# Two of four token groups loaded later, one more up-projection block ahead of the spectral part, and transposes dealt out singly

## The chip, the cores and the metric

The kernel runs on one core of a Trainium2 chip. The core has a matrix engine (PE in the profile; its weight loads are PEld), a vector engine (DVE), a scalar engine (ACT) and a general engine (POOL); SP does no arithmetic and issues most of the transfers. SP, POOL and ACT each have an in-order queue of instructions, and so have PE and DVE: an instruction that waits holds up all that stand behind it on the same engine. The metric is the device time of one execution in microseconds (us), as the median of several runs.

## The reference

The program computes the forward pass and all gradients of one conditioned transformer block with a spectral mixer. Sequence S = 2048, width D = 1024, hidden width F = 3584, bf16 tensors. Cut to what matters:

```
mod = (silu(c) @ w_mod)                      # six rows of D: sa, ca, ga, sb, cb, gb
h   = layernorm(x) * (1 + ca) + sa
x1  = x + ga * irfft2(rfft2(h) * (A_w_r + 1j * A_w_i))
h2  = layernorm(x1) * (1 + cb) + sb
out = x1 + gb * (gelu(layernorm(h2) @ B_w1 + B_b1) @ B_w2 + B_b2)
_out, _vjp = jax.vjp(f, A_x, A_w_r, A_w_i, B_w1, B_b1, B_w2, B_b2, c, w_mod)
return _out, *_vjp(grad_out)
```

So there are three layer norms (n1 inside h, n2 inside h2, n3 in front of the MLP), one forward and one backward two-dimensional transform, and the products of the MLP: `z = n3 @ w1`, `gelu(z) @ w2`, and backward `ph = (gb * grad_out) @ w2^T`, `gz @ w1^T`, and the two weight gradients.

## The kernel before, in words

Tokens are held in four groups of 512 (four tiles of 128 rows each). x lies in the tiles `x4s[0..3]`, grad_out in `gos[0..3]`. A group of x is loaded by `load_tok` (L142): one plain transfer of 512 KB that SP issues, and two gathers of 256 KB each that POOL issues, because half of a group's rows are taken in reversed order.

The start of the program (L356 to L372) is a list of loads on SP: x 0, the two halves of w_mod's row ca (`mod_get(1, h)`), x 1 between them, x 2, x 3, the two halves of row gb (`mod_get(5, h)`), grad_out 0, two transposed blocks of w2 (`load_w2t`), grad_out 1 to 3, two more w2 blocks. The tiles for blocks of w_mod are a ring of three, so the second half of gb waits for the first product. A modulation row half is eight matmuls of PE (`mod_block`, L273) and a copy out of PSUM.

Then come the statistics of the first layer norm: group 1 on ACT (`ln_act`), groups 0, 2 and 3 on DVE (`ln_dve`: eight bn_stats and four aggregations a group). Each ends in a Sqrt on ACT. `x_sqrt` keeps these four instructions; the Sqrt of groups 2 and 3 is tied behind the last Sin of the transform matrices (`behind(x_sqrt[k], trig_in[0])`), since Sqrt and Sin need different ACT tables. `norm_act` (L419) writes the normed rows into `fbuf`.

Next, grad_out is transposed on PE, four 128x128 pieces to a PSUM bank (`pt`, L472), and copied out scaled by gb into `gBoT`, even banks by DVE (L476), odd ones by ACT (L480). After each of the four groups come the products of the first two w2 blocks with it (`ph_part`, L450; a part is eight matmuls, a block of four parts 32 matmuls, copied out by ACT or DVE and stored to `d_ph`). There are 28 such blocks (NFC). `PH_EARLY = 7` says that blocks 0 to 7, eight in all, are placed ahead of the spectral part; the last matmul of them is `early_pe`, behind which the first spectral matmuls `pu` (L581) are tied. `gen_mats` (L540) makes the transform matrices: POOL works out indices in `gidx`, DVE masks them, ACT takes the Sin. It stands behind the products of row sa (`mod_block(0, h)`). Meanwhile DVE folds the four normed groups (L880 to L891: multiply with 1 + ca, fold the tokens, fold the columns); the spectral part needs the result of all four.

The spectral part (`spectral_core`) is a chain of products on PE and long elementwise work on DVE. The remaining ph blocks follow it in the program, and their matmuls are also set between the spectral ones. Its last step, `consume_fwd` (L901), makes from each of four groups the output of the transform, x1, the second norm and n3; DVE carries most of it. When block `N3_AT` (23) is done, group 0 of n3 is turned (L951 to L964): eight banks of four 128x128 transposes, `pn`, in the PSUM pools s and d of two banks each, copied out into `n3Ta` alternately by DVE (`dve_copy`, L848) and ACT (`s_copy`, L845). The odd copies are ordered ahead of a Sqrt (`behind(n3_sqrts[2], ...)`). Blocks 24 to 27 then run their first halves, and `z_block` begins: `pz` (L1009) takes n3Ta and w1.

The order on each engine is set in advance by a scheduler: among the instructions that it takes to be ready it issues the one earliest in the program, `tc.high_priority()` puts the copies out of PSUM first, `tc.issue_after` and `ordered()` fix an order on one engine, and `nc.any` leaves the choice between ACT and DVE to it. On the chip this order is kept whether or not it fits the real times.

Of the kernel before, what the change touches and what calls it, by code (L numbers as in the profile page):

```python
# [22 lines left out]
NDC = D // P  # L23
# [12 lines left out]
def kernel(  # L36
# [105 lines left out]
    def load_tok(t4, src, i, eng=None):  # L142
        s3 = tok_flat(src)
        ins = (eng or nc.sync).dma_start(out=tok_plain(t4, i), in_=tok_rows(s3, i, 0, D))
        for q in range(2):
            nc.gpsimd.indirect_dma_start(out=t4[:, tok_idx(i, q), :], out_offset=None, in_=s3,
                                         in_offset=bass.IndirectOffsetOnAxis(ap=xidx[:, 2 * i + q:2 * i + q + 1], axis=0))
        return ins
# [211 lines left out]
    mod_get(1, 0)  # L360
    load_tok(x4s[1], A_x, 1)
    mod_get(1, 1)
    load_tok(x4s[2], A_x, 2)
    load_tok(x4s[3], A_x, 3)
    mod_get(5, 0)
    for h in range(2):
        mod_block(1, h, wm[1, h][:])
# [10 lines left out]
    def ln_act(x4, row, i, jk):  # L378
        sv = small.tile([P, 4, 4], FP32, tag="lnsv")
        for q in range(4):  # L380
            nc.scalar.activation(out=jk[:, q, :], in_=x4[:, q, :], func=ACT.Identity, accum_out=sv[:, q, 0:1])
        nc.vector.tensor_scalar(out=sv[:, :, 1:2], in0=sv[:, :, 0:1], scalar1=-1.0 / D, scalar2=None, op0=ALU.mult)
        for q in range(4):
            nc.scalar.activation(out=jk[:, q, :], in_=x4[:, q, :], func=ACT.Square, bias=sv[:, q, 1:2], accum_out=sv[:, q, 2:3])
        ln_fin(sv[:, :, 2:3], sv[:, :, 1:2], sv[:, :, 3:4], 1.0 / D, row, i)
# [7 lines left out]
    def ln_dve(x4, row, i):  # L393
        st = small.tile([P, 4, 2, nc.vector.BN_STATS_DIM], FP32, tag="lnst", bufs=1)
        mv = small.tile([P, 4, 4], FP32, tag="lnmv")
        for q in range(4):
            for h in range(2):
                nc.vector.bn_stats(out=st[:, q, h, :], in_=x4[:, q, h * KH:(h + 1) * KH])
            nc.vector.bn_aggr(out=mv[:, q, 0:2], in_=st[:, q])
        nc.vector.tensor_scalar(out=mv[:, :, 2:3], in0=mv[:, :, 0:1], scalar1=-1.0, scalar2=None, op0=ALU.mult)  # L400
        ln_fin(mv[:, :, 1:2], mv[:, :, 2:3], mv[:, :, 3:4], 1.0, row, i)
# [23 lines left out]

    sqrt_in, norm_in = [None], [()]

    x_sqrt = []
    for i in range(4):
        if i == 1:  # L430
            ln_act(x4s[i], 0, i, fbuf[:, i])
        else:
            with tc.issue_after(u_in.ins):
                ln_dve(x4s[i], 0, i)
        x_sqrt.append(sqrt_in[0])
    for i in range(2):
        norm_act(fbuf[:, i], x4s[i], 0, i)
    pc = ps_d("pc")
# [84 lines left out]
    def trig(dst, colv, rowv, nrow, width, modn, cosine):  # L523
        idx = gidx[:, gcount[0] % 2, :]
        gcount[0] += 1
        sh = float(3 * modn // 4 if cosine else modn // 2)
        for r in range(nrow):
            ov = idx[:, r * width:(r + 1) * width]
            pts(ov.rearrange("p (s w) -> p s w", s=2) if len(colv.shape) == 3 else ov, colv, rowv[r], sh, ALU.mult, ALU.add)
        n = nrow * width  # L530
        nc.vector.tensor_scalar(out=idx[:, 0:n], in0=idx[:, 0:n], scalar1=modn - 1, scalar2=None, op0=ALU.bitwise_and)
        with tc.issue_after(x_sqrt[1].ins):
            trig_in[0] = nc.scalar.activation(out=dst, in_=idx[:, 0:n].rearrange("p (r w) -> p r w", w=width), func=ACT.Sin,
                                 bias=negpi[:], scale=2 * np.pi / modn)

# [4 lines left out]
    def gen_mats():  # L540
        for cl, colv, modn in ((CE, kev, 2048), (SE, kev, 2048), (CO, kod, 4096), (SO, kod, 4096)):
            sm = (smA, smB)[cl % 2]
            rows, n = (rowo, 4) if cl % 2 else (rowe, 2)
            if cl == SE:
                nc.gpsimd.memset(kev[:, 0:1], 512.0)
            for r in range(0, n, 2):
                trig(sm[:, cl // 2, r:r + 2, :], colv, rows[r:r + 2], 2, 512, modn, cl < 2)
            if n == 2:
                nc.gpsimd.dma_start(out=d_SF[:, cl, 0:n], in_=sm[:, cl // 2])
        for cl, colv, modn in ((CE, jf[:, 0:256], 1024), (SE, jf[:, 1:257], 1024), (CO, jod, 2048), (SO, jod, 2048)):  # L550
            trig(em1[:, 0, 2 * cl:2 * cl + 2, :], colv, rowe, 2, 256, modn, cl < 2)
        for k in (2, 3):
            behind(x_sqrt[k], trig_in[0])
        for k in range(2):
            with tc.issue_after(x_sqrt[1].ins):
                nc.scalar.activation(out=al[:, k, :], in_=rown, func=ACT.Sin, scale=np.pi / (2048 << k))
        nc.scalar.mul(out=em1[:, 1], in_=em1[:, 0], mul=2.0 / (S * D))
        nc.gpsimd.tensor_scalar(out=em1[:, 1, 0:2, 0:1], in0=em1[:, 0, 0:2, 0:1], scalar1=1.0 / (S * D), scalar2=None, op0=ALU.mult)
        nc.gpsimd.tensor_scalar(out=em1[:, 1, 4:6, 255:256], in0=em1[:, 0, 4:6, 255:256], scalar1=1.0 / (S * D), scalar2=None, op0=ALU.mult)
        nc.gpsimd.dma_start(out=d_E[:], in_=em1[:])  # L560

    def behind(ins, later):
        tc.add_manual_dep(ins.ins, later.ins.name, mybir.DependencyInfo(mybir.DependencyClass.NoSync, mybir.DependencyReason.DATA),
                          reason="order")
# [279 lines left out]
    def s_copy(out, in_):  # L844
        return nc.scalar.copy(out=out, in_=in_)  # L845

    def dve_copy(out, in_):
        nc.vector.tensor_copy(out=out, in_=in_)  # L848


    for h in range(2):
        wm[0, h] = mod_tile()
        mod_load(0, h, wm[0, h][:], nc.sync)
        with ordered():
            mod_block(0, h, wm[0, h][:])
    gen_mats()
    gb2s = small.tile([P, NDC], FP32, tag="u_rt", bufs=1)
    nc.vector.reduce_sum(out=gb2s[:], in_=gu[:, 0:4, :].rearrange("p j c -> p c j"), axis=AX.X)
    gb2_bf = small.tile([P, NDC], BF16, tag="gc_bf", bufs=1)
# [8 lines left out]

    phs.append(reg.tile([P, 4, BW], BF16, name="phr", tag="ph")[:])

    PH_EARLY = 7
    late_mods = [(r, h) for r in (2, 3, 4) for h in range(2)]
    for fc in range(PH_EARLY):
        if fc > 1:
# [26 lines left out]
    def consume_fwd(i, o4, tmp, tmp2, x4, eb):  # L901
        unfold_d(o4, tmp)
        unfold_tok(o4, tmp)
        nc.gpsimd.dma_start(out=chunk_rows(d_A, i), in_=o4)
        load_tok(x4, A_x, i, nc.gpsimd)
        tt(tmp, o4, bcn(ga_row, 4), ALU.mult)
        tt(x4, tmp, x4, ALU.add)
        nc.gpsimd.dma_start(out=chunk_rows(d_x1, i), in_=x4)
        ln_mix(x4, 1, i, tmp)
        norm_act(tmp, x4, 1, i)  # L910
        tt(tmp, tmp, bcn(opcb_row, 4), ALU.mult)
        tt(tmp, tmp, bcn(sb_row, 4), ALU.add)
        ln_dve(tmp, 2, i)
        n3_sqrts.append(sqrt_in[0])
        n3 = tmp
        if i < 2:
            n3 = reg.tile([P, 4, D], BF16, name=f"n3_{i}", tag=f"uv{i}")
            n3h.append(n3)
        if i < 3:
            norm_act(n3, tmp, 2, i)  # L920
        else:
            for q in range(4):
                t = 4 * i + q
                nc.vector.tensor_scalar(out=tmp[:, q, :], in0=tmp[:, q, :], scalar1=stats[:, 2, 0, t:t + 1],
                                        scalar2=stats[:, 2, 1, t:t + 1], op0=ALU.mult, op1=ALU.add)
        (nc.scalar if i < 3 else nc.sync).dma_start(out=chunk_rows(d_n3, i), in_=n3)

    n3h, n3_sqrts = [], []
    spectral_core(True, fbuf, (smA, smB), em1[:, 1], [css[:, 0], css[:, 1]], new_pair_temps(PXT[2:6]),
                  act_copy, act_copy, act_copy, consume_fwd, "fr")  # L930

# [10 lines left out]
            w1s.append(wtile)  # L942

    PH_KEEP = NFC - 4
    N3_AT = PH_KEEP - 1
    for fc in range(PH_EARLY + 1, NFC):
        if fc >= PH_EARLY + 4:
            load_w2t(fc)
            load_w1({24: 1, 25: 1, 27: 5}.get(fc, 0))
        ph_part(fc, (0, 1, 2, 3) if fc < PH_KEEP else (0, 1))  # L950
        if fc == N3_AT:  # L951
            n3Ts = [reg.tile([P, NDC, BW], BF16, name="n3Ta", tag="uv3")]
            for cch in range(NDC):
                pt = (ps_s, ps_d)[cch % 2]("pn")
                for q in range(4):
                    with ordered():
                        last_pn = nc.tensor.matmul(pt[:, q * P:(q + 1) * P], lhsT=n3h[0][:, q, cch * P:(cch + 1) * P], rhs=ident,
                                                   start=True, stop=True)
                with tc.high_priority():
                    if cch % 2:  # L960
                        behind(n3_sqrts[2], s_copy(n3Ts[0][:, cch, :], pt[:]))
                    else:
                        dve_copy(n3Ts[0][:, cch, :], pt[:])
            last_pe[0] = last_pn  # L964

    hhA = reg.tile([P, 8, 4, BW], BF16, name="hhA", tag="fr")
    uvp0 = reg.tile([P, 2, 4, BW], BF16, name="hhB", tag="uv0")
# [763 lines left out]
```

## Time and profile before

| what | value |
|---|---|
| median of 3 runs | 1397.15 us (1394.73 to 1397.84) |
| profiled execution, its own time | 1392.75 us |
| span of the profiled execution | 1391.0 us |
| PE busy | 1357.8 us, 98% |
| DVE busy | 1065.4 us, 77% |
| ACT busy | 768.7 us, 55% |
| POOL busy | 352.1 us, 25% |
| transferred | 330.08 MB, 237 GB/s on the mean |

The span runs from the first to the last instruction; the execution's own time has 1.75 us around it. PE is busy nearly always, and the places where it isn't can be counted: a view of waits says for an engine what it waited for, how long and how often; a timeline lists instructions in order, with the idle time before each in square brackets; a view by windows gives each engine's busy time in a stretch, with the clock that PE was granted in it (1.00 is full) and the share in which the transfer engines were busy.

### The profile page before, as it was taken

What the parts mean: (1) busy time and instruction counts of PE and PEld (TensorE: products, weight loads), DVE (VectorE), ACT (ScalarE), POOL (GpSimd) and SP (SyncE); (2) the same over time, 40 slices, a digit from 0 to 9 for tenths busy, and PEclk for the clock granted to TensorE, in tenths of its full rate; (3) what the DMA queues carried; (4) which work ended last, traced back from release to release, by engine and by line L of the source; (5) the groups of instructions that cost most, each with busy time, mean ns of one, the idle gap of its engine ahead of it and who ended that gap; (6) DMA issues with size and microseconds to landing.
All of it is one profiled execution on the core that took longest, in us unless ns stands there. A gap on an engine that the chain in (4) does not pass through costs nothing. (4 is left out here: it accounts for less than half of the span.)

```text
span 1391.0 us, 18668 instructions
## 1 busy us (share of the span) xinstructions
PE 1357.8 (98%) x6931; PEld 655.6 (47%) x6931; DVE 1065.4 (77%) x1471; ACT 768.7 (55%) x1090; POOL 352.1 (25%) x438
## 2 busy tenths in 40 slices
PE   4999999989999999999999999999999999999999
PEld 2445675444444444444444444444555555454444
DVE  5997889996788787787811388789887588967990
ACT  5865756657877765756503684446633464544311
POOL 4421622210112122122111011111344320332341
PEclk8999999999999999999999999999999999999999
DMA  9994657898887786597899779998669968799991
GB/s 327 278 243 113 174 132 237 239 277 288 250 253 240 218 270 230 196 274 251 247 314 234 208 186 264 284 299 235 217 214 258 237 149 256 213 251 218 309 342 68
DMA packets 356178, 330.08 MB, mean 237 GB/s; under 512 B 203835, under 2 KB 298449, under 8 KB 355959
## 3 DMA queue, kind: packets, MB, share of 16 engines
q1 hardware_dynamic: 313990, 200.76, 56.4%
q0 software_dynamic: 35328, 120.26, 25.5%
q10 hardware_dynamic: 6768, 7.87, 1.7%
q8 instruction: 54, 0.88, 0.3%
q14 instruction: 38, 0.30, 0.1%
HBM read 165.73 MB, written 114.87 MB: 202 GB/s over the span
## 5 line engine op out<-in xcount | busy, mean ns | idle before, releaser
L456 PE MATMUL pp<-gBoT,wt 128*128 128x512 bf16 x896 | 200.1, 381 | 0.6 <-DVE gBoT L476 0.3
L1163 PE MATMUL pg<-w1T,gzr 128*128 128x512 bf16 x896 | 196.0, 379 | 2.2 <-DMA gzr<-d_gz 2.2
L1599 PE MATMUL gw1acc<-gzh,n3n 128*128 128x512 bf16 x640 | 139.6, 379 | 0.0
L1163 PEld LDWEIGHTS <-gzr 128*128 128x128 bf16 x896 | 86.5, 98 | 110.9 <-issue 5.8
L1009 PEld LDWEIGHTS <-w 128*128 128x128 bf16 x896 | 87.2, 98 | 106.8 <-issue 2.3
L1599 PEld LDWEIGHTS <-n3n 128*128 128x128 bf16 x896 | 87.4, 98 | 105.2 <-issue 1.3
L456 PEld LDWEIGHTS <-wt 128*128 128x128 bf16 x896 | 87.7, 98 | 103.4 <-issue 3.5
L1009 PE MATMUL pz<-n3Tb,w 128*128 128x512 bf16 x448 | 99.2, 379 | 0.9 <-DVE w2sD L1085 0.9
L1009 PE MATMUL pz<-n3Ta,w 128*128 128x512 bf16 x448 | 98.7, 379 | 0.0
L195 DVE TENSOR_TENSOR ct<-ct 128x2048 bf16<-128x2048 bf16 (+1 forms) x84 | 91.5, 1117 | 5.1 <-ACT n L423 2.5
L1012 ACT ACTIVATE gt<-pz,b_col 128x512 bf16<-128x512 f32 x112 | 73.6, 684 | 38.3 <-PE pz L1009 37.9
L1063 PEld LDWEIGHTS <-hhA 128*128 128x128 bf16 x608 | 59.1, 98 | 71.6 <-issue 1.4
L1335 PE MATMUL gw2acc<-gB,hhsA 128*128 128x512 bf16 x416 | 92.4, 379 | 0.0
L1603 ACT CAST gwo<-gw1acc 128x512 bf16<-128x512 f32 x56 | 32.2, 582 | 107.7 <-PE gw1acc L1599 89.9
L1020 ACT ACTIVATE gt<-gt 128x2048 bf16<-128x2048 bf16 x28 | 53.5, 1911 | 60.6 <-DVE gt L195 60.6
L195 DVE TENSOR_TENSOR gt<-gt,gt 128x2048 bf16<-128x2048 bf16 x56 | 68.5, 1224 | 19.2 <-ACT gt L1022 17.8
L1343 ACT CAST gwo<-gw2acc 128x512 bf16<-128x512 f32 x40 | 23.6, 589 | 87.4 <-PE gw2acc L1335 75.9
L1335 PEld LDWEIGHTS <-hhsA 128*128 128x128 bf16 x416 | 40.6, 98 | 47.2
L1599 PE MATMUL gw1acc<-gzu,n3n 128*128 128x512 bf16 x256 | 55.4, 379 | 0.0
L1016 ACT ACTIVATE gt<-gt 128x2048 bf16<-128x2048 bf16 x28 | 53.5, 1909 | 2.1 <-DVE hhC L195 1.3
L1022 ACT ACTIVATE gt<-gt 128x2048 bf16<-128x2048 bf16 x28 | 53.4, 1907 | 0.4
L462 ACT CAST pho<-pp 128x512 bf16<-128x512 f32 x61 | 34.4, 584 | 33.1 <-PE pp L456 32.5
(380 smaller groups left out, 2538.5 us busy)
## 6 DMA issues: line engine op xcount, KB each, us to landing
gzr<-d_gz SPq DMA_DIRECT2D x28, 512.0 KB
wblk<-in_w_mod_dram SPq DMA_DIRECT2D x12, 1024.0 KB
d_ph<-pho POOLq DMA_DIRECT2D x21, 512.0 KB
out_dram<-otl POOLq DMA_DIRECT2D x40, 256.0 KB
d_hh<-hhA POOLq DMA_DIRECT2D x19, 512.0 KB
wrw<-in_w_mod_dram SPq DMA_DIRECT2D x32, 256.0 KB
out_dram<-gwo POOLq DMA_DIRECT2D x57, 128.0 KB
w<-in_B_w_dram SPq DMA_DIRECT2D x7, 1024.0 KB
```

Of the source, the lines that this page charges most:

```text
L195: return nc.vector.tensor_tensor(out=out, in0=a, in1=b, op=op)
L456: last_pe[0] = nc.tensor.matmul(pp[:], lhsT=wt[:, fc % 4, cch, :], rhs=gBoT[j][:, cch, :], start=(cch == 0), stop=(cch == NDC - 1))
L462: nc.any.tensor_copy(out=ov, in_=pv)
L1009: last_pe[0] = nc.tensor.matmul(pz[:], lhsT=w1s[g][:, cch, k * P:(k + 1) * P], rhs=n3T[:, cch, :], start=(cch == 0), stop=(cch == NDC - 1))
L1012: z_in = nc.scalar.activation(out=zb[:, k, :], in_=pz[:], func=ACT.Identity, bias=b1_col[:, fc:fc + 1], scale=1.0)
L1016: nc.scalar.activation(out=av, in_=zb, func=ACT.Square)
L1020: nc.scalar.activation(out=sg, in_=bv, func=ACT.Sigmoid, scale=2.0 * GK)
L1022: nc.scalar.activation(out=bv, in_=bv, func=ACT.Sigmoid, scale=-2.0 * GK)
L1063: last_pe[0] = nc.tensor.matmul(pbs[i][:], lhsT=hh[:, k, i * P:(i + 1) * P], rhs=wp[:, k, :], start=False, stop=(g == 6 and k == 3))
L1163: last_pg[0] = nc.tensor.matmul(pgs[i][:], lhsT=gzs[b, g][:, k, i * P:(i + 1) * P], rhs=w1Ts[g][:, k, h * KH:(h + 1) * KH], start=(g == 0 ...
L1335: nc.tensor.matmul(acc[:], lhsT=hh_of(fc)[:, t, :], rhs=gBs[t // 4][:, t % 4, h * KH:(h + 1) * KH], start=(t == 0), stop=(t == NT - 1))
L1599: nc.tensor.matmul(acc[:], lhsT=n3ns[t // 4][:, t % 4, cch * P:(cch + 1) * P], rhs=gz2[t // 8][:, t % 8, :], start=(t == 0), stop=(t == NT ...
```

## The change

It has three parts.

- The loads of x 2 and x 3 leave the list at the start and come behind `gen_mats()`, which itself moves ahead of the products of row sa. With them go `ln_dve` of groups 2 and 3, whose Sqrt stays behind the last Sin (`issue_after(trig_in[0])`, in place of `behind`). Of the first group pair, `ln_act` of group 1 now stands before `ln_dve` of group 0 in the program.
- `PH_EARLY` becomes 8: blocks 0 to 8 of ph stand ahead of the spectral part, and one block more of w2 is loaded there.
- The turning of n3's group 0 begins at block 21 (`PH_KEEP - 3`) in place of 23, and one bank is turned after every half block: six times in blocks 21 to 23, twice behind the first halves of 24 and 25. Even banks are now copied by ACT, odd ones by DVE, and the order ahead of the Sqrt is dropped.

```diff
     mod_get(1, 1)
-    load_tok(x4s[2], A_x, 2)
-    load_tok(x4s[3], A_x, 3)
     mod_get(5, 0)
...
-    x_sqrt = []
-    for i in range(4):
-        if i == 1:
-            ln_act(x4s[i], 0, i, fbuf[:, i])
-        else:
-            with tc.issue_after(u_in.ins):
-                ln_dve(x4s[i], 0, i)
-        x_sqrt.append(sqrt_in[0])
+    ln_act(x4s[1], 0, 1, fbuf[:, 1])
+    with tc.issue_after(u_in.ins):
+        ln_dve(x4s[0], 0, 0)
+    x_sqrt = sqrt_in[0]
...
-        for k in (2, 3):
-            behind(x_sqrt[k], trig_in[0])
...
+    gen_mats()
+    for i in (2, 3):
+        load_tok(x4s[i], A_x, i)
+    for i in (2, 3):
+        with tc.issue_after(trig_in[0].ins):
+            ln_dve(x4s[i], 0, i)
     for h in range(2):
         wm[0, h] = mod_tile()
...
-    gen_mats()
...
-    PH_EARLY = 7
+    PH_EARLY = 8
...
-    N3_AT = PH_KEEP - 1
+    N3_AT = PH_KEEP - 3
+    n3Ts, n3_turned = [], [0]
     for fc in range(PH_EARLY + 1, NFC):
...
-        ph_part(fc, (0, 1, 2, 3) if fc < PH_KEEP else (0, 1))
         if fc == N3_AT:
             n3Ts = [reg.tile([P, NDC, BW], BF16, name="n3Ta", tag="uv3")]
-            for cch in range(NDC):
+        for js in ((0, 1), (2, 3)) if fc < PH_KEEP else ((0, 1),):
+            ph_part(fc, js)
+            if n3Ts and n3_turned[0] < NDC:
+                cch = n3_turned[0]
+                n3_turned[0] += 1
                 pt = (ps_s, ps_d)[cch % 2]("pn")
                 for q in range(4):
                     with ordered():
                         last_pn = nc.tensor.matmul(pt[:, q * P:(q + 1) * P], lhsT=n3h[0][:, q, cch * P:(cch + 1) * P], rhs=ident,
                                                    start=True, stop=True)
+                last_pe[0] = last_pn
                 with tc.high_priority():
-                    if cch % 2:
-                        behind(n3_sqrts[2], s_copy(n3Ts[0][:, cch, :], pt[:]))
-                    else:
-                        dve_copy(n3Ts[0][:, cch, :], pt[:])
-            last_pe[0] = last_pn
+                    (s_copy, dve_copy)[cch % 2](n3Ts[0][:, cch, :], pt[:])
```

More of the change, by code (lines that the diff above doesn't have):

```diff
@@ L531, in trig @@
         nc.vector.tensor_scalar(out=idx[:, 0:n], in0=idx[:, 0:n], scalar1=modn - 1, scalar2=None, op0=ALU.bitwise_and)
-        with tc.issue_after(x_sqrt[1].ins):
+        with tc.issue_after(x_sqrt.ins):
             trig_in[0] = nc.scalar.activation(out=dst, in_=idx[:, 0:n].rearrange("p (r w) -> p r w", w=width), func=ACT.Sin,
@@ L551, in gen_mats @@
             trig(em1[:, 0, 2 * cl:2 * cl + 2, :], colv, rowe, 2, 256, modn, cl < 2)
-        for k in (2, 3):
-            behind(x_sqrt[k], trig_in[0])
         for k in range(2):
-            with tc.issue_after(x_sqrt[1].ins):
+            with tc.issue_after(x_sqrt.ins):
                 nc.scalar.activation(out=al[:, k, :], in_=rown, func=ACT.Sin, scale=np.pi / (2048 << k))
@@ L913, in consume_fwd @@
         ln_dve(tmp, 2, i)
-        n3_sqrts.append(sqrt_in[0])
         n3 = tmp
@@ L926, in consume_fwd @@
         (nc.scalar if i < 3 else nc.sync).dma_start(out=chunk_rows(d_n3, i), in_=n3)
-    n3h, n3_sqrts = [], []
+    n3h = []
     spectral_core(True, fbuf, (smA, smB), em1[:, 1], [css[:, 0], css[:, 1]], new_pair_temps(PXT[2:6]),
```

## The prediction, made before the result was known

> **What bounds the kernel now.** I read the page first, for the share of each engine.
>
> ```profile
> span 1391.0 us, 18668 instructions
> PE 1357.8 (98%) x6931; PEld 655.6 (47%) x6931; DVE 1065.4 (77%) x1471; ACT 768.7 (55%) x1090; POOL 352.1 (25%) x438
> ```
>
> PE is the bound. The change adds and takes away no matmul, so it can only act on PE's 33.2 us of idle time (1391.0 - 1357.8) and on matmuls that ran at a lower clock. Second I read PE's waits, from the start to 60 us and from 214 to 330 us, the stretches that the change touches (us in total, times, longest).
>
> ```profile
> PE pm L279 <- DMA wblk<-in_w_mod_dram: 14.2, 3, 6.5
> PE pt L472 <- ACT gBoT L480: 2.8, 5, 1.6
> ...
> PE pn L957 <- DVE n3Ta L848: 4.4, 1, 4.4
> ```
>
> Third, PE's timeline there (start, length, instruction, count, idle before).
>
> ```profile
> 15.88 3.43 PE L279 MATMUL pm<-wblk,u_b 128*128 128x512 bf16 x8 [3.49 <-DMA wblk<-in_w_mod_dram]
> 23.59 6.40 PE L279 MATMUL pm<-wblk,u_b 128*128 128x512 bf16 x16 [4.29 <-DMA wblk<-in_w_mod_dram]
> ...
> 30.11 0.28 PE L472 MATMUL pt<-ident,go 128*128 128x128 bf16 x2
> ...
> 58.03 3.62 PE L279 MATMUL pm<-wblk,u_b 128*128 128x512 bf16 x16
> ...
> 100.39 13.98 PE L456 MATMUL pp<-gBoT,wt 128*128 128x512 bf16 x64
> 114.20 1.04 PE L581 MATMUL pu<-smA,fbuf 128*128 128x256 bf16 x8
> ...
> 301.70 1.06 PE L957 MATMUL pn<-ident,n 128*128 128x128 bf16 x16
> ...
> 308.53 0.38 PE L957 MATMUL pn<-ident,n 128*128 128x128 bf16 x4 [4.42 <-DVE n3Ta L848]
> ...
> 323.82 7.07 PE L1009 MATMUL pz<-n3Ta,w 128*128 128x512 bf16 x32
> ```
>
> The reader is to see the marks: the row gb at 23.59, grad_out's transposes from 30.11, the end of its four groups at 58.03, the spectral part at 114.20, n3's turns from 301.70 to 309, z at 323.82.
>
> **Part 1: n3's turns dealt out.** Four banks are turned at once; the later ones need a copy first, and DVE's comes late. DVE's timeline, and two windows (PE, PEld, DVE, ACT, POOL busy, then PE's clock, transfer share, GB/s):
>
> ```profile
> 303.28 2.27 DVE L195 TENSOR_TENSOR ct<-ct,rows 128x4096 bf16<-128x4096 bf16 x1
> ...
> 305.59 2.29 DVE L195 TENSOR_TENSOR xt<-ct,xt 128x4096 bf16<-128x4096 bf16 x1
> 307.80 1.88 DVE L848 CAST n3Ta<-pn 128x512 bf16<-128x512 f32 x3
> ```
>
> ```profile
> 303.90:308.50 4.60, 0.21 (x1) 0.00 (x0) 4.60 (x5) 0.54 (x1) 0.33 (x1) 1.00 1.04 279
> 308.50:312.60 4.10, 4.07 (x18) 1.90 (x18) 3.33 (x9) 2.80 (x7) 0.44 (x1) 0.58 1.02 316
> ```
>
> The copies stood behind two long products. PE stood for 4.42 us, and in the next 4.10 us its clock was 0.58, which lost 4.10 x 0.42 = 1.7 us more. Dealt out, a turn comes every half block: two blocks take 114.20 - 100.39 = 13.8 us, so a block 6.9, a half 3.45. A bank is wanted again four turns on, 13.8 us later, against a copy that was 307.80 - 301.70 = 6.1 us behind the first transpose. The wait goes: -4.4 - 1.7 = -6.1 us. It can't gain more; it gains nothing if the wait comes back in front of z. The eighth copy becomes DVE's, and only the half blocks of 26 and 27 (6.9 us) stand between its turn and z, so its cover is 0.8 us.
>
> [...]
>
> **Part 2: x 2 and x 3 out of the way.** From 14 to 19 us the transfer view shows POOL's queue (q0) and SP's (q1) side by side: packets, MB, share of the engines.
>
> ```profile
> q0 software_dynamic: 311, 1.05, 54.1%
> q1 hardware_dynamic: 517, 0.92, 50.1%
> ```
>
> That is 1.97 MB, nearly the two groups whole (two plain transfers of 512 KB, four gathers of 256 KB), in 5.0 us at a full share. Without them gb's halves land 5.0 us sooner. The first product of gb could start at 23.59 - 5.0 = 18.6, but PE is busy with row ca until 15.88 + 3.43 = 19.3; so 4.3 us sooner, and grad_out's transposes at 30.11 - 4.3 = 25.8.
>
> From there PE isn't alone. The window 30 to 58, and ACT's groups from 26 to 55.3 us (count, busy us, mean ns, idle before):
>
> ```profile
> 30.00:58.00 28.00, 23.67 (x200) 14.25 (x201) 27.77 (x60) 25.54 (x49) 7.11 (x10) 1.00 0.87 269
> ```
>
> ```profile
> L480 ACT ACTIVATE gBoT<-pt,gb_col 128x512 bf16<-128x512 f32 x16 | 10.8, 688 | 1.9 <-PE pt L472 1.9
> L423 ACT ACTIVATE fbuf<-x,stats 128x1024 bf16<-128x1024 bf16 x8 | 9.7, 1240 | 0.0
> ...
> L462 ACT CAST pho<-pp 128x512 bf16<-128x512 f32 x4 | 2.4, 588 | 0.3 <-PE pp L456 0.3
> ```
>
> PE's own work there is 23.7 us, so it could end at 25.8 + 23.7 = 49.5 and, with waits like the present 4.3, at 53.8 for 58.0. But ACT was idle for only 1.9 + 0.3 = 2.2 us; in its present order it ends no more than 2.2 sooner. DVE lightens it: the statistics that leave are
>
> ```profile
> L398 DVE BATCH_NORM_STATS2 st<-x 128x6 f32<-128x512 bf16 x16 | 10.2, 666 | 0.0
> ...
> L399 DVE BATCH_NORM_AGGREGATE mv<-st 128x2 f32<-128x12 f32 x8 | 1.6, 196 | 0.0
> ```
>
> 11.8 us between 20 and 42 us, room for ACT's four casts (2.4 us). So the gain is between 2.2 and 4.6, with 4.3 from PE's side; I take 3.5, the middle, since nothing binds the casts to DVE. Below nothing it goes only by the first rival.
>
> The moved transfers. The plain halves (1 MB, 2.7 us at 1.97 MB in 5.0 us) now stand on SP in front of row sa's blocks, whose issues were
>
> ```profile
> 41.20 2.73 SPq L271 DMA_DIRECT2D wblk<-in_w_mod_dram x3
> ```
>
> and whose use was at 58.03: 14 us of cover; without it PE waits one for one. On POOL the four gathers pass the index work of the matrices:
>
> ```profile
> 13.55 0.95 POOL L146 DMA_INDIRECT x<-in_A_x_dram,xu  x1 [0.31 <-issue]
> ...
> 46.38 0.64 POOL L549 DMA_DIRECT2D d_SF<-smA  x1 [26.48 <-ACT smA L533]
> ```
>
> Each takes 1.25 us with the gap, 5.0 in all, and POOL stood idle for 26.5 us there: no cost, if they are set into that gap. Nothing puts them behind grad_out on another queue. Should they run early, beside gb and grad_out, they take half the engines again, and 2.6 of the 5.0 us (1.05 MB at 1.97 MB in 5.0 us) are lost: grad_out starts at 27.7. ACT's end is then still the later one, so the sum stays.
>
> [...]
>
> The other moves are of order only: `gen_mats` ahead of row sa, group 1's statistics ahead of group 0's. Each engine keeps the same instructions, and row sa's use at 58.03 leaves the 14 us named; without that cover the delay counts one for one.
>
> **Part 3: nine blocks ahead.** A block of 6.9 us moves in front of the spectral part, for PE at no cost. It covers DVE, which now does the 11.8 us of statistics where it was already full:
>
> ```profile
> 41.50:111.00 69.50, 67.06 (x355) 31.82 (x353) 66.55 (x96) 47.01 (x75) 26.42 (x33) 1.00 0.85 241
> ...
> 109.75 1.22 DVE L195 TENSOR_TENSOR fbuf<-fbuf,x 128x2048 bf16<-128x2048 bf16 x1
> ```
>
> The folds ended at 109.75 + 1.22 = 111.0. Of the 11.8, DVE's idle 69.50 - 66.55 = 2.95 take some, and a group's four copies of gBoT (3 us at 0.75) move ahead of the stretch: 111.0 + 11.8 - 3 - 3 = 116.8. PE is ready at 114.20 + 6.9 - 3.5 = 117.6. So DVE hides behind the block with 0.8 us to spare, and I take nothing; if the folds are later, PE waits one for one, 0 to 4 us. On SP one load of a w2 block more stands ahead of the spectral part's:
>
> ```profile
> 114.39 1.24 SPq L342 DMA_TRANSPOSE wt<-in_B_w_dram  x1
> 125.22 6.13 SPq L735 DMA_TRANSPOSE smi<-d_SF  x4
> ```
>
> It waits for PE to free its buffer, a block after this one (114.39 + 6.9 - 3.5 = 117.8), and its 1.24 us end before the next issue: no cost.
>
> The spectral part then starts 3.4 us later than now and z 9.6 us sooner (6.1 + 3.5), so the work of n3's last groups on DVE and ACT reaches 13 us further into z. ACT shows what that means:
>
> ```profile
> 323.10 0.30 ACT L388 ACTIVATE mv<-mv,eps_c 128x4 f32<-128x4 f32 x1 [2.59 <-DVE mv L416]
> ```
>
> ACT waits there for DVE, 2.59 us, and behind such a wait would now stand the copies of pz, with four banks of 1.7 us in reserve (7.07 us for four). Cost 0 to 4.4 us, the upper end that of the stall of today; I take 1.0, near the reserve's side.
>
> **Sum.** -6.1 - 3.5 + 0 + 1.0 = -8.6 us. The profiled execution took 1392.75 us (span 1391.0 and 1.75 around it), which gives 1384.2. The median of the runs, 1397.15, stands 4.4 us above that execution; with the same difference the forecast is 1388.5.
>
> **The rivals.** First, the slower one: DVE waits in its queue for x 2. The planner may set its bn_stats among the copies of gBoT, as it does now:
>
> ```profile
> 34.79 1.28 DVE L398 BATCH_NORM_STATS2 st<-x 128x6 f32<-128x512 bf16 x2
> ```
>
> If POOL gathers behind the work that waits until 46.38 (3.5 sooner then, 42.9, and two gathers of 1.25 and their transfer of half a MB, 1.3), x 2 is whole at about 47. From 35 on DVE stands for 12 us, the copies of gBoT behind it, and PE with them. For it: the gathers stand late in the program; against: POOL was idle long before. Price: a stop S costs S, and 1.7 for the clock behind it: -8.6 + 12 + 1.7 = +5.1, 1402.3. It decides from S = 6.9, and can be measured from 9.7.
>
> Second, part 2 is hidden anyway: ACT keeps its order, or DVE's folds eat the gain in front of the spectral part. Then only the turns count: -6.1 + 1.0, 1392.
>
> Third, the turn's wait returns before z, DVE being 13 us further behind: +6.1, so -3.5 + 1.0 = -2.5, 1394.6.
>
> **How the numbers follow.** The forecast has 0.50, the first rival 0.22, the second 0.18, the third 0.10. What a measurement can tell from no change is 0.2%, 2.8 us. The forecast's own range runs from the best ends (-6.1 - 4.6) to the worst (-6.1 - 2.2 + 4.4), with the 1.6 us by which the runs spread: 1384.8 to 1394.9. Faster: 0.50 + 0.18 and no part of the third, 0.68; same: the third, 0.10; slower: 0.22. To leave out no more than 2 in 10 the range goes from 1384.8 to 1400, into the lower part of the slower case.
>
> **What would show it.** The wait of pn gone, one turn after each half block, no clock below 1 around 300 us. pm of gb at about 19.3, transposes of grad_out at 26 to 28, row sa at 54.5, pu at 117.6. Wrong if DVE has an idle time that x's transfer ended between 30 and 55 us, if pu waits for a fold, or if pz waits for n3Ta or for ACT.

## The result and the profile after

The changed kernel took 1387.63 us (median of 6 runs, 1385.91 to 1390.13); the kernel before, timed beside it, 1394.81 (median of 6, 1390.79 to 1397.84). The ratio is 0.9949, with a 95% interval of 0.993 to 0.9968: faster, by 4 to 10 us, less than 1%. The forecast was 1388.5. The profiled execution took 1387.2 us, 5.6 less than that of before, and its page begins with

```profile
span 1385.4 us, 18669 instructions
...
PE 1357.9 (98%) x6931; PEld 655.6 (47%) x6931; DVE 1067.4 (77%) x1477; ACT 765.1 (55%) x1084; POOL 357.4 (26%) x438
```

PE's work is what it was; its idle time went from 33.2 to 27.5 us. Where, PE's timeline of the changed kernel tells (start, length, instruction, count, idle before):

```profile
26.03 0.29 PE L466 MATMUL pt<-ident,go 128*128 128x128 bf16 x2 [0.47 <-DMA go<-in_grad_out_dram]
...
49.55 0.27 PE L466 MATMUL pt<-ident,fbuf 128*128 128x128 bf16 x2 [1.76 <-DVE gBoT L470]
...
51.47 4.92 PE L450 MATMUL pp<-gBoT,wt 128*128 128x512 bf16 x16
...
56.23 3.62 PE L279 MATMUL pm<-wblk,u_b 128*128 128x512 bf16 x16
...
66.37 0.22 PE L210 MATMUL ptr<-ident,gb_bf 128*8 128x128 bf16 x1 [1.34 <-DVE gb_bf L857]
...
120.18 1.04 PE L573 MATMUL pu<-smA,fbuf 128*128 128x256 bf16 x8
...
309.11 0.39 PE L957 MATMUL pn<-ident,n 128*128 128x128 bf16 x4
...
316.24 7.07 PE L1006 MATMUL pz<-n3Ta,w 128*128 128x512 bf16 x32
...
439.10 2.86 PE L1006 MATMUL pz<-n3Tb,w 128*128 128x512 bf16 x8 [2.25 <-DVE w2sD L1082]
441.75 4.37 PE L1060 MATMUL pbo<-w2sC,hhC 128*128 128x512 bf16 x16
445.96 6.21 PE L1006 MATMUL pz<-n3Tb,w 128*128 128x512 bf16 x28
```

Two rows of the kernel before belong beside the last three:

```profile
445.36 1.89 PE L1009 MATMUL pz<-n3Tb,w 128*128 128x512 bf16 x8 [0.93 <-DVE w2sD L1085]
...
450.53 1.67 PE L1009 MATMUL pz<-n3Tb,w 128*128 128x512 bf16 x7
```

Mark by mark, after against before (the marks of before stand in the prediction):

| mark | before | after | difference |
|---|---|---|---|
| grad_out's first transpose | 30.11 | 26.03 | -4.08 |
| row sa | 58.03 | 56.23 | -1.80 |
| spectral part, less the block of 6.9 moved ahead of it | 114.20 | 120.18 - 6.9 | -0.92 |
| first pz | 323.82 | 316.24 | -7.58 |
| pz behind the bank pa | 450.53 | 445.96 | -4.57 |
| span | 1391.0 | 1385.4 | -5.6 |

In this pair of executions the start wins 4.1 us and keeps 0.9 of them. The turns win 6.7 more (7.58 - 0.92), and the wait of pn has gone; the last turn at 309.11 has no idle time in front of it. At 439 the kernel gives 3.0 us back. The 1.0 us won later comes from a shorter wait for a transfer, less 0.3 lost on the way: pg's wait for gzr, 2.2 us before, is now

```profile
PE pg L1160 <- DMA gzr<-d_gz: 0.8, 1, 0.8
```

How the start lost its gain is in DVE's timeline of the changed kernel:

```profile
45.16 1.88 DVE L396 BATCH_NORM_STATS2 st<-x 128x6 f32<-128x512 bf16 x3 [1.03 <-DMA x<-in_A_x_dram]
...
47.62 1.21 DVE L195 TENSOR_TENSOR x<-fbuf 128x2048 bf16<-128x2048 bf16 x1
48.74 0.75 DVE L470 TENSOR_SCALAR_CACHE_REDUCE gBoT<-pt,gb_col 128x512 bf16<-128x512 f32 x1
...
117.67 0.69 DVE L195 TENSOR_TENSOR fbuf<-fbuf,sb_saf 128x1024 bf16<-128x1024 bf16 x1
```

DVE stands 1.03 us for a plain half of x, which SP issued late, behind two blocks of w2:

```profile
27.60 10.91 SPq L342 DMA_TRANSPOSE wt<-in_B_w_dram  x2
38.55 1.09 SPq L144 DMA_DIRECT2D x<-in_A_x_dram  x2
```

Then DVE works off statistics and a fold, and only then makes the copy of gBoT at 48.74 for which PE has waited 1.76 us. The last fold ends at 117.67 + 0.69 = 118.36, ahead of PE's need at 120.18.

### The profile page after: what moved, and what is told of

It is laid out like the page before. It is cut to its first block, busy times and chain, and to the rows that moved or that the text cites. A ratio compares the mean times of both kernels' runs of the same rounds, so it can differ in the third digit from the quotient of the medians.

```text
span 1385.4 us, 18669 instructions
## 1 busy us (share of the span) xinstructions
PE 1357.9 (98%) x6931; PEld 655.6 (47%) x6931; DVE 1067.4 (77%) x1477; ACT 765.1 (55%) x1084; POOL 357.4 (26%) x438
## 5 line engine op out<-in xcount | busy, mean ns | idle before, releaser
L1332 PE MATMUL gw2acc<-gB,otl 128*128 128x512 bf16 x224 | 50.0, 379 | 0.0
```

The costliest lines, as they stand in the source:

```text
L1332: nc.tensor.matmul(acc[:], lhsT=hh_of(fc)[:, t, :], rhs=gBs[t // 4][:, t % 4, h * KH:(h + 1) * KH], start=(t == 0), stop=(t == NT - 1))
```

## The experiments

The runs of one kernel spread by some 10 us (before: 1388.7 to 1399.2 in 31 runs of one batch). So each experiment is read twice: by its ratio, and by the marks of its profile, where an edit shows at its place.

**e1_turns: the turns alone, on the kernel before.**

```diff
-    N3_AT = PH_KEEP - 1
+    N3_AT = PH_KEEP - 3
...
+        for js in ((0, 1), (2, 3)) if fc < PH_KEEP else ((0, 1),):
+            ph_part(fc, js)
+            if n3Ts and n3_turned[0] < NDC:
...
-                    if cch % 2:
-                        behind(n3_sqrts[2], s_copy(n3Ts[0][:, cch, :], pt[:]))
-                    else:
-                        dve_copy(n3Ts[0][:, cch, :], pt[:])
+                    (s_copy, dve_copy)[cch % 2](n3Ts[0][:, cch, :], pt[:])
```

> Part 1 alone on the kernel before: turns from block 21, one bank after each half block. Theory (the wait and the lower clock behind it are what is gained): no wait of pn, z begins 6 to 6.7 us sooner than the kernel before; PE then meets the copy of pa into w2sD at 440 us earlier than DVE and waits there 2 to 3 us more, clock loss included, so the time is 3.5 to 5 us shorter. Rival (the wait only moves): pz waits for n3Ta or for ACT by 4 us or more at the start of z, and the time is unchanged.

Measured: 1389.44 us, ratio 0.9984 (0.9964 to 1.0003); span 1384.0. From the first pu to the first pz it took 315.85 - 112.55 = 203.3 us; before, 323.82 - 114.20 = 209.6. That is 6.3 us, with no wait of pn left: the term of the turns. Its row sa stands at

```profile
56.42 3.62 PE L279 MATMUL pm<-wblk,u_b 128*128 128x512 bf16 x16
```

1.61 us ahead of before, though no instruction up to there differs. e4, e5, e11 and e12 share these instructions too, and with them row sa stands anywhere from 56.42 to 58.26 (e4). So a mark in the first 60 us says nothing below 1.8 us, and the 1.80 of the changed kernel is no more than that. The turns alone also bring the wait of 2.06 us at 438.51; it belongs to them and not to the other parts. The marks came as the theory had them; the 3.5 to 5 us did not, for the medians differ by 2.2, and the interval includes 1.

**e2_start: the later x 2 and x 3 alone, on the kernel before.**

```diff
     mod_get(1, 1)
-    load_tok(x4s[2], A_x, 2)
-    load_tok(x4s[3], A_x, 3)
...
+    gen_mats()
+    for i in (2, 3):
+        load_tok(x4s[i], A_x, i)
+    for i in (2, 3):
+        with tc.issue_after(trig_in[0].ins):
+            ln_dve(x4s[i], 0, i)
```

> Part 2 alone (x 2 and x 3 later, eight blocks ahead as before). Theory: grad_out's transposes begin 4 us sooner, at 58 us only about 2 are left, and the folds on DVE end at 118 us, 4 to 5 us after PE is ready for the spectral part; n3's turns wait for DVE as before or longer. Time 4 to 7 us longer than before. Rival (DVE's later folds are hidden): the spectral part begins at 113 us and the time is 1 to 2 us shorter.

Measured: 1395.94 us, ratio 1.0023 (1.0002 to 1.0044). PE's waits of this kernel:

```profile
PE pu L573 <- DVE fbuf L195: 2.0, 1, 2.0
...
PE pn L954 <- DVE n3Ta L840: 4.6, 1, 4.6
```

Without the ninth block DVE's folds end behind PE, and pu waits for them: 2.0 us, where the theory had 4 to 5. The start alone costs (4.2 us by the medians, at the lower edge of the theory's 4 to 7), and the block is the cover it needs.

**e4_nine: the ninth block alone, and e3_start_nine: the block with the later x 2 and x 3.** Both are made on the kernel before, with its old turns; e3 adds the edit of e2.

```diff
-    PH_EARLY = 7
+    PH_EARLY = 8
```

> Part 3 alone: nine blocks ahead, loads as before. PE's work ahead of the spectral part grows by 6.9 us, which begins at 121 us. Theory: the wait of pn grows by up to those 6.9, to about 11 us, and the time is 5 to 8 us longer; the wait for the copy of pa at 445 us goes, DVE having caught up while PE stood. Rival: DVE has slack in between, the wait stays at 4.4 and the time is unchanged.

> Parts 2 and 3 without the dealt turns. Theory: the spectral part begins at 120 us without a wait, so the work of n3 on DVE lies some 6 us later against PE, and the wait of pn for DVE's copy grows from 4.4 to about 10 us, with 1.7 us for the clock: time 3 to 6 us longer than before. Rival (the turns' wait hangs on nothing but the number of banks): the wait stays near 4.4, time 1 us shorter than before.

Measured: e4 1394.38 us, ratio 1.0009 (0.9989 to 1.0029); e3 1392.34, ratio 1.0005 (0.998 to 1.0031). Neither is told apart from no change. In both the turn's wait stayed as it was; e3's row, which e4's answers with the same 4.2:

```profile
PE pn L954 <- DVE n3Ta L840: 4.2, 1, 4.2
```

The theory that the wait grows by what the spectral part comes later is wrong. From pu to pz e4 takes 203.1 us and e3 203.0, which with the block of 6.9 is 210.0, as before. The copies follow the turn in the order of DVE's queue, and it seems that the whole queue moves with PE. e4's theory also missed the copy of pa: PE still waits 0.90 us for it, for 0.93 before.

**e5_act_copies and e12_act_copies: the kernel before, all eight copies of the turned banks made by ACT.** One line; the turns stay where they were.

```diff
-                    if cch % 2:
-                        behind(n3_sqrts[2], s_copy(n3Ts[0][:, cch, :], pt[:]))
-                    else:
-                        dve_copy(n3Ts[0][:, cch, :], pt[:])
+                    behind(n3_sqrts[2], s_copy(n3Ts[0][:, cch, :], pt[:]))
```

> The kernel before, with all eight turned banks copied by ACT and none by DVE, all turns still in one place. Theory (DVE's queue is late, its copies stand behind two products of 2.3 us): the wait of pn falls from 4.4 to at most 1.5 us in pieces, no lower clock behind it, z begins 4.5 to 6 us sooner. Rival (four banks for eight turns are too few for any engine): pn waits 3 us or more, for ACT.

Measured in e5: one execution of 1390.92 us beside 1389.41 of the kernel before. The wait of pn is gone; ACT's timeline of e5 has all eight copies in one group:

```profile
301.23 4.02 ACT L845 CAST n3Ta<-pn 128x512 bf16<-128x512 f32 x8
```

From pu to pz it takes 316.84 - 113.18 = 203.7 us, 5.9 less than before. So what PE waited for was DVE's queue and nothing else: no turn had to be moved for the gain. In this execution the gain was lost again behind z, in waits for hhsA (2.4 us) and gn3a (1.6). The same kernel in more runs:

> The kernel before with all eight turned banks copied by ACT, in more runs. Theory: the turn's wait is a matter of DVE's queue alone, so taking DVE out gives what dealing the turns out gives: z some 5.8 us sooner, no wait of pn, a ratio of 0.996 to 0.998; the waits for hhsA (2.4 us) and gn3a (1.6) of its first profile belong to that execution. Rival: ACT's four more copies (2.4 us) come back as those waits behind z, and the ratio is 0.999 or more, as in its single run (1390.9 for 1389.4).

Measured in e12: 1386.21 us, ratio 0.9954 (0.9938 to 0.9971), span 1384.9. Again 5.9 us from pu to pz (317.50 - 113.81 = 203.7); the wait for hhsA is 1.1, that for gn3a is gone. And the pz behind pa waits no longer than before:

```profile
439.04 1.89 PE L1006 MATMUL pz<-n3Tb,w 128*128 128x512 bf16 x8 [0.93 <-DVE w2sD L1082]
```

The theory held, with a ratio a little better than it had. One changed line does what the whole change does.

**e6_stats_behind: the changed kernel, with the statistics of x 2 and x 3 behind DVE's last copy of gBoT.**

```diff
+                    gb_last[0] = nc.vector.tensor_scalar(out=gBoT[j][:, cch, :], in0=pt[:], ...
...
-        with tc.issue_after(trig_in[0].ins):
+        with tc.issue_after(trig_in[0].ins), tc.issue_after(gb_last[0].ins):
             ln_dve(x4s[i], 0, i)
```

> The changed kernel, with the bn_stats of x 2 and x 3 ordered behind DVE's last copy of gBoT. Theory (the start's gain was lost where DVE waited for x 2 at 44 to 45 us with copies of gBoT behind it): the wait of 1.8 us at 49.5 goes and with it the lower clock from 50.8 to 55, the end of the four groups comes at 52.5 to 53.5 in place of 56.2, and DVE's folds stay hidden or cost 1 to 2 us in front of the spectral part. Rival (ACT and DVE are full anyway): other waits of pt take its place and the end stays within 0.7 of 56.2.

Measured: 1391.6 us, span 1389.8. Row sa came at 52.40, 3.83 us sooner than in the changed kernel (and no wait of pt is longer than 0.5 us): the stop for x 2 and what stood behind it were the loss at 49. But none of it lasts. PE's waits of e6, and DVE's last fold:

```profile
PE ptr L210 <- DVE gb_bf L858: 2.4, 1, 2.4
PE pu L574 <- DVE fbuf L195: 1.8, 1, 1.8
```

```profile
121.55 0.69 DVE L195 TENSOR_TENSOR fbuf<-fbuf,sb_saf 128x1024 bf16<-128x1024 bf16 x1
```

The fold ends at 122.24, 3.9 us later than in the changed kernel, pu waits for it, and the first pz stands at 316.48 for 316.24. From about 49 us to the spectral part DVE has no room: from 70 to 118 us it is busy for 48.0 of 48.0 us in the changed kernel and for 47.8 in e6. What it doesn't do early it does late, and PE pays either at 49 or at 120. (Of the fold's 3.9 us, three copies out of PSUM that fell to DVE in place of ACT in e6 make 2.0; the rest stays open.) Of the 4.4 us by which e6's span is the longer, 4.0 are lost near the end, around a wait of 2.2 us of gw1acc for ACT, where no instruction of the edit stands (the mean clock over the span is 0.996, for 0.998 in the changed kernel).

**e7_gathers_late: the changed kernel, with x 2 and x 3 gathered behind the first store of the matrices.** This makes the prediction's first rival true.

```diff
-                nc.gpsimd.dma_start(out=d_SF[:, cl, 0:n], in_=sm[:, cl // 2])
+                sf_in.append(nc.gpsimd.dma_start(out=d_SF[:, cl, 0:n], in_=sm[:, cl // 2]))
...
-        load_tok(x4s[i], A_x, i)
+        with tc.issue_after(sf_in[0].ins):
+            load_tok(x4s[i], A_x, i)
```

> The changed kernel, with POOL's four gathers of x 2 and x 3 ordered behind the first store of the matrices (32 us) in place of 12 to 20 us. Theory (half of the transfer engines went to the gathers between 16 and 24 us): the second half of gb and grad_out land 1.5 to 2.5 us sooner, grad_out's transposes begin at 24 to 25 us in place of 26.0; x 2's gathered rows come at 38 to 42 us, so the wait of DVE at 44 to 45 does not grow by more than 1 us. The slower rival of the prediction: DVE stops for the gathered rows for 4 us or more with copies of gBoT behind it, and the end of the four groups comes later than 58 us.

Measured: 1399.46 us, span 1397.7. DVE stands for x, and the copy of pho that PE's transposes wait for stands behind it (DVE's row, then PE's):

```profile
40.04 1.29 DVE L396 BATCH_NORM_STATS2 st<-x 128x6 f32<-128x512 bf16 x2 [5.04 <-DMA x<-in_A_x_dram,xu]
```

```profile
41.97 0.37 PE L466 MATMUL pt<-ident,fbuf 128*128 128x128 bf16 x2 [3.74 <-DVE pho L456]
```

The theory was right about grad_out, whose transposes begin at 24.25, 1.78 sooner than in the changed kernel. It was wrong about DVE: the stop is 4.0 us longer than the changed kernel's 1.03, row sa comes at 58.28, and the first pz at 319.90, 3.66 later: nearly one for one. (The other 8.6 us of the span came later, in waits of 5.4 us for gn3a and 3.1 for hhsA, which the changed kernel's profile doesn't have.) So the early place of the gathers, which the trace after confirms (the last is issued at 18.67 us), is what kept the rival small.

**e8_pa_first and e10_after_pa: the changed kernel, DVE's copy of the bank pa one place earlier in its queue.** Both are the same kernel.

```diff
-                nc.vector.tensor_copy(out=gacc[:, cs_], in_=pa[:])
+                pa_in = nc.vector.tensor_copy(out=gacc[:, cs_], in_=pa[:])
+                if h == 0:
+                    behind(hh_tts[9], pa_in)
```

The copy stood behind a product for which DVE itself waits for ACT, as these rows of the changed kernel's DVE show:

```profile
437.22 1.23 DVE L195 TENSOR_TENSOR hhA<-gt,gt 128x2048 bf16<-128x2048 bf16 x1 [1.25 <-ACT gt L1017]
438.36 0.69 DVE L1082 COPY w2sD<-pa 128x512 f32<-128x512 f32 x1
```

It stood in the same place in the kernel before:

```profile
443.48 1.22 DVE L195 TENSOR_TENSOR hhA<-gt,gt 128x2048 bf16<-128x2048 bf16 x1 [1.25 <-ACT gt L1020]
444.62 0.68 DVE L1085 COPY w2sD<-pa 128x512 f32<-128x512 f32 x1
```

So the change didn't make this place. PE's z comes 7.58 us sooner than before, this product on DVE only 6.26, and PE's wait grows by the difference, from 0.93 to 2.25 us. In e12 PE wins 6.32 at z and the product 6.33 (it starts at 437.15), and the wait stays at 0.93.

> The changed kernel, with DVE's copy of pa into w2sD set one instruction earlier, ahead of the product that waits for ACT's Sigmoid. Theory (PE waits 2.25 us at 437 to 439 for that copy alone, and loses 1.7 us more to the lower clock behind it): the wait falls under 0.5 us, the clock stays at 1, and everything behind comes 3 to 4 us sooner. Rival (the MLP's elementwise chain bounds that stage, PE is only ahead of it): another wait of 1.5 us or more comes within 100 us behind.

> The changed kernel with DVE's copy of pa one place earlier, as e8. In e8 z came 10 us late, behind a wait of 7.6 us for wt, so that DVE had caught up before the copy; its vanished wait is no proof yet. Theory A: the 2.25 us at 439 are that place in DVE's queue; with z in time the wait of pz for w2sD is at most 0.5 us and 2 to 4 us are gained, 1.5 to 3.5 at the end. Theory B: the earlier place only looked good behind the late z; 1.5 us or more of the wait stay and the time is e9's within 1 us. On wt: if the 7.6 us belong to the one execution, they're not in this profile and the median isn't above e9's; if they belong to the kernel, they return and the median is 5 us above.

Measured: e8 1401.52 us in one execution; e10 1388.38, ratio 0.9974 (0.9951 to 0.9997). In both profiles the wait for w2sD is gone, and from the first pz to the one behind pa the kernel wins 4.1 us against the changed kernel (10.29 - 6.19 in e8, 12.69 - 8.59 in e10). But in both z came late, behind a wait for a block of w2 that the changed kernel doesn't have. From e10's waits, and from the transfers of e10 and of the changed kernel between 309 and 314 us:

```profile
PE pp L450 <- DMA wt<-in_B_w_dram: 8.5, 1, 8.5
```

```profile
DMA packets 257, 0.35 MB, mean 71 GB/s; under 512 B 165, under 2 KB 186, under 8 KB 257
```

```profile
DMA packets 971, 2.03 MB, mean 405 GB/s; under 512 B 45, under 2 KB 620, under 8 KB 971
```

No instruction ahead of 430 us differs in order, yet the transfers crawl. They do so from about 285 us on, as the last section shows. Of e10's 12 runs four took over 1392 us (1392.92 to 1398.96), of the changed kernel's 9 beside it none. What stops the transfers stays open. With z late DVE had caught up, so these two runs don't prove what the copy's place is worth.

**e11_turns_pa: the turns alone with the copy of pa one place earlier.** It is e1 with the edit of e8.

> The turns alone with the copy of pa one place earlier; against the run before this one it is without the moved x 2 and x 3 and the ninth block. Theory: those two are worth 0.9 us by the marks, so this stands 0 to 1.5 us above that run. Rival 1: they cost, as the start alone did (1395.9 for 1391.7), and this is 1 to 3 us below. Rival 2: they're worth the 3.5 us of the prediction, and this is 2.5 us or more above.

Measured: 1387.0 us, ratio 0.9965 (0.9947 to 0.9984), span 1384.1. Here z came in time (316.79), and the pz that waited 2.06 us in e1 runs through:

```profile
432.04 7.08 PE L1010 MATMUL pz<-n3Tb,w 128*128 128x512 bf16 x32
```

So the wait at 439 goes with that one place in DVE's queue. At the end nothing of it is seen: gw2acc waits 2.2 us for hhsA. And against e10 the kernel without the later x 2 and x 3 and without the ninth block is 1.4 us faster, which is what the first rival had, but with intervals that overlap widely, and four of e10's runs are the long ones above. This pair shows no gain from the two parts, where the prediction gave them 3.5 us.

**e9_after: the changed kernel again, beside e10 to e12.**

> The changed kernel again, beside the three below on one chip. Theory: the turns give 6.6 us at z, the start 0.9, and of that some 2 are lost behind z, so 4 to 6 us by the marks and a ratio of 0.993 to 0.997. Rival: what e1 showed for the turns alone over ten runs (2.2 us, 0.9984) is all that lasts; then 0.997 to 1.000.

Measured: 1387.48 us for 1391.65 of the kernel before, ratio 0.9957 (0.9937 to 0.9977), span 1383.8, as the theory had it. Of the four kernels timed together e12 has the lowest median; their intervals all overlap.

## Why the prediction was right, and where it wasn't

**The turns, -6.1: right.** They measured 6.3 alone and 6.7 in the change, 5.9 by e5's and e12's other way. The mechanism was the one named, copies behind two long products in DVE's queue: taking DVE out removes the wait without moving a turn.

**The start, -3.5: wrong, it is nothing.** The step that failed is "the gain is between 2.2 and 4.6", which weighed PE's and ACT's idle time and took DVE for lightened, and with it "below nothing it goes only by the first rival". The transposes did start 4.1 us sooner, for 4.3 worked out, but that is luck: the 4.3 had the gathers in POOL's gap, and for gathers beside gb the prediction gave 27.7. They ran beside gb, and the first transpose came at 26.03; with the gathers late it came at 24.25 (e7). So they cost 1.8 us and not 2.6, and without them the start would have come 5.9 sooner. What follows is decided by DVE's queue. ACT did hand casts to DVE, as hoped (the page of the profile after has six instructions fewer on ACT and six more on DVE), but the statistics came back among the copies of gBoT. The prediction counted what x's plain halves hold up on SP, not what holds them up: two blocks of w2 whose issues took 10.91 us. So the first rival came in small, with the prediction's own sign of it, an idle time of DVE that x's transfer ended (1.03 us, then a statistic and a fold, 1.76 us on PE with 1.6 lost to the clock behind it, 0.36 of 4.5 us); then PE waited 1.34 at gb_bf. At the spectral part the five executions with the later x 2 and x 3 and the ninth block, its own gathers and statistics in place (e3, the changed kernel, e8, e9, e10), begin at 119.76 to 121.53, 120.5 on average; the five with the old start and eight blocks (before, e1, e5, e11, e12) at 112.55 to 114.20, 113.4 on average, with a block 120.4. The term measures 0, and as each five spread over 1.7 us, a gain of well under 1 us could hide in it.

**The ninth block, 0: right, and needed.** The folds ended at 118.36, 1.6 later than the 116.8 worked out; PE came at 120.18 and not at 117.6, because the start gained less, so the cover was 1.8 us. e2 shows the price where it is gone: 2.0 us of wait.

**z, +1.0: the size was too small and the place was wrong.** No copy of pz waited at z's start. The loss is at 439, where DVE's copy of pa stands behind a product that waits for ACT: 1.3 us more wait (2.25 for 0.93) and 1.7 of clock; 1.0 came back by gzr. That DVE falls behind a PE that comes sooner was part of the mechanism named; it shows some 120 us later than expected. e1 shows that the turns alone bring it. Why DVE's product wins only 6.26 us isn't shown.

**The rivals.** The second, that only the turns count, is what happened by mechanism; its -5.1 is nearer to the profiled 5.6 than the sum is, and its 1392 came from the high reference of 1397.15. The third fell with the profile after, where no matmul waits between the turns and z, and in e3 and e4 the wait didn't grow.

**The sum.** It gave -8.6. The two profiled executions differ by 5.6, the medians by 7.2 and, in the second comparison, by 4.2. That 1387.63 fell so near to 1388.5 is luck: the sum was 3.0 us too large, and the reference of 1397.15 was 2.3 above the 1394.81 timed beside the changed kernel, with which the sum would have given 1386.2. The 3.0 us between the sum and the profiled difference are the start's 2.6 and one more at z, less 0.6 that the turns gave beyond their term.

## What to carry to other kernels

Before work is dealt out over a loop because an engine waits for copies, look at whose queue the copies stand in: giving them to the other engine was one line here and worth about the same (5.9 us from pu to pz in e12, 6.3 by dealing out in e1). An engine that is not the bound of the kernel can be the bound of a stage (DVE, 77% of the span, was busy for 48.0 of 48.0 us from 70 to 118 us); there a gain at the stage's start is only kept if that engine's total work gets less or has time after it. And a place behind an instruction that itself waits for another engine is a costly one in a queue: the bank that held PE up at 439 needed one place, not a faster copy (2.06 us of wait in e1, none in e11).

## What the runs showed of the hardware

**After a gap of 2.25 us TensorE's clock fell in one execution, after one of 2.24 us in another it didn't.** Behind the same wait at 439 us the changed kernel's window (its columns as in the prediction) and that of its repetition e9:

```profile
439.10:446.00 6.90, 6.90 (x25) 2.77 (x25) 6.21 (x6) 4.36 (x6) 3.04 (x3) 0.75 0.92 275
```

```profile
439.10:446.00 6.90, 6.80 (x32) 3.13 (x32) 6.65 (x7) 4.46 (x6) 2.72 (x3) 1.00 0.85 284
```

The drop costs 6.9 x 0.25 = 1.7 us, and e9's span is 1.6 shorter. In the changed kernel the gap and the half clock behind it lie in these two stretches:

```profile
436.45:439.86 3.41, 1.16 (x6) 0.48 (x5) 2.53 (x3) 3.38 (x4) 1.22 (x3) 1.00 0.53 158
439.86:443.27 3.41, 3.41 (x10) 1.18 (x8) 3.31 (x4) 2.24 (x4) 1.39 (x1) 0.50 0.93 228
```

It was the same elsewhere: after 1.76 us at 49.55 the clock was 0.64 over the next 4.5 us, after 1.90 in e9 it was 1.00, and after 2.67 at 439 in e6 it was 1.00 as well. The turn's gaps of 4.2 to 4.6 us were followed by a lower clock each time: 0.58 over 4.10 us in the kernel before, 0.50 in e2 from 309.7 to 313, in e3 from 305.4 to 309.4 and in e4 from 307 to 311.

So the length alone doesn't tell, in these runs, which gap of about 2 us the clock falls behind, and what does is not shown. Twelve gaps of 1.73 to 2.67 us, in the changed kernel and in e1, e2, e6, e7, e9 and e10, have a window of 3.7 to 6.9 us read behind them: in five it is at 0.61 to 0.75, in seven at 1.00. In a sum a gap of 2 us should then carry somewhat less than half of the 1.7 us, about 0.7 (an estimate from these twelve).

**In e10 the transfers crawled for several microseconds with the engines shown as busy.** There 0.35 MB moved between 309 and 314 us where the changed kernel moved 2.03 MB. The packets of POOL's and SP's queues took 80.2% and 29.8% of the engines' time in e10, 70.4% and 33.4% in the changed kernel. POOL's queue there, in e10 and in the changed kernel (packets, MB, share):

```profile
q0 software_dynamic: 72, 0.29, 80.2%
```

```profile
q0 software_dynamic: 380, 1.44, 70.4%
```

These are packets of about 4 KB, and one took 0.89 us on the mean for 0.15 (share x 16 engines x 5.0 us, over their number). It began earlier, as a window of both, in the same order, shows:

```profile
285.00:290.00 5.00, 5.00 (x28) 2.40 (x27) 2.54 (x5) 4.96 (x6) 0.54 (x1) 1.00 1.25 84
```

```profile
285.00:290.00 5.00, 5.00 (x28) 2.38 (x27) 2.54 (x3) 4.63 (x7) 0.36 (x1) 1.00 1.09 329
```

SP then needed 9.74 us to issue the block of w2 at 288.42, for 1.24 at 287.06 in the changed kernel. The runs don't show why the transfers were slow.
